# A fused windowed attention and FFN kernel: who sets the ones tile, and the order of loads, units and first FFN chunks in the first half batch

## The chip, the cores and the metric

The kernel runs on one core of a Trainium2 chip. The metric is the device time in microseconds of one execution, as the median of some runs. A profile is one such execution, taken by the hardware profiler; its span reaches from the first instruction to the last and leaves out what lies around it.

Names of the engines in the profile: PE does matmuls and transposes (PEld is its weight load), DVE is VectorE, ACT is ScalarE, POOL is GpSimd, SP only issues DMAs here. ACT and POOL issue some DMAs too.

## The reference

```python
def _attn_ref(q, k, v, n_sink, window):          # q, k, v: (4, 8, 768, 64); n_sink 4, window 128
    scores = 1.0 / np.sqrt(D) * np.matmul(q, k.transpose(0, 1, 3, 2))
    keep = is_sink | in_window                   # key < 4, or 0 <= query - key < 128
    scores = np.where(keep, scores, -1000000000.0)
...
    a = np.exp(scores)
    a = a / (np.sum(a, axis=-1, keepdims=True) + 1e-09)
    return np.matmul(a, v)

def _moe_ref(x, w_in, w_out, beta):              # x: (3072, 512), w_in: (512, 2048), w_out: (2048, 512)
    h = x @ w_in
    g = h * (1.0 / (1.0 + np.exp(-beta * h)))
    return g @ w_out
```

The attention's output, heads side by side, is x. Inputs and the output are float32.

## The kernel before

The work is cut into eight half batches of 384 tokens, and each of these into four units of two heads. A unit passes these steps: its q and k are cast to bfloat16 and transposed on PE (T, line 795, copied out to qkT by ACT or DVE); scores of a burst of tiles (S, line 895) and their exponential on ACT (E, line 913); probabilities times values and the division (A, lines 1000 to 1006); the transpose of the result into xT (R, line 1026). In the first half batch the mask is a bias that PE adds to the scores (line 876); from the second on it is set on E after the exponential, by POOL (line 927) or DVE (lines 921 and 931). From the fourth half batch on the transposes T and R are done by DMA and not by PE. A half batch's x then goes through the FFN: H (line 1053) is four matmuls that make a 128x384 tile of h, followed by tanh on ACT (t, line 1063) and a product on DVE (g, line 1065); O (line 1081) multiplies four g tiles with w_out. Outputs are copied to osb and stored from POOL's queue (line 1099).

In the first half batch values come in another layout, so that they are sorted by nine matmuls with one-hot matrices (V, line 705), of which POOL first casts the values (mix, tile g, line 567). The first four FFN tiles of that half batch (w_in columns 0 to 511) are not made one after the other, but as P0 to P3: P with number c adds the contribution of heads 2c and 2c+1 to all four. They need the weight chunks w0 and w1. B brings the beta of the FFN in.

All PE work stands in one list. For the first half batch this list is written out by hand in `ENTRY` (T0 S0 V0 and so on), for the rest in `ORDER`, one letter each. Where the inputs' loads of the first half batch stand is told by `LOAD0`, the loads that come next (chunks w0 to w7 of w_in, and q, k and three pieces v of the second half batch) by `FIRST`. The loads of q and v of the first half batch are issued by SP, its k by ACT, all else by SP. A planner (`Graph`) then lays out casts, copies and masks on ACT, DVE and POOL by estimated costs (the `ns` of each operation, landings of DMAs from `NQ0`, `NV0` and a list of stalls), and each engine's instructions are written out in the order that the planner gave, with semaphores between them. Which engine does a cast or a copy, and in which order an engine does its work, thus follows from the planner's estimates. No time on the chip does.

Where the planner expects PE to wait in the first half batch, it puts in fillers (line 1301): matmuls of the ones tile with itself, 512 or 256 columns wide, into a bank that nobody reads. The ones tile is written by POOL (line 576), after one of the kS tiles and the bias tiles (lines 588 to 600); identity, one-hot and mask tiles are derived from it. ACT's first activation (line 623) reads it too. Stalls and costs stand in lines 51, 61 and 211, the estimates of the first loads in line 485, the loads themselves in lines 656 and 668. Casts and copies have one helper, so that they stand in lines 565 (ACT), 567 (POOL) and 570 (DVE), told apart by their tiles.

Of the kernel before, what the change touches and what calls it, by code (L numbers as in the profile page):

```python
# [9 lines left out]
B, H, S, D = 4, 8, 768, 64  # L10
# [9 lines left out]
EW = 256 * (NB - 1) + 128  # L20


ENTRY = "T0 S0 V0 T1 S1 V1 T2 S2 A0 A1 V2 V3 A2 R0 T3 S3 R1 P0 A3 B R2 P1 R3 P2 P3"
FIRST = "w0 w1 q k w3 w2 w5 w4 v1 v2 v0 w6 w7"
ORDER = "THHTTTHASHHHSHHSHAHHHAHHOROHOHHRHAHRTROHOAOHSORTOSOOATHOTHHOOHHHOSOHHOHOHRAAARAOHRROSOOHHHAHSOOHHOOHAHHRHHROHRHOROOSRAOOSOOOOHHOHAARHHHHAHOHRHHHHHHOHOOSOOHOHHOOHHSOHOHHHHHHROHHOARSAORHRAORAOOOSOAOROOHHHHHHHHROHOHHHHHHHHRHHHHHHHHOOOOOSOOOOOHHSHHHARHOOHHHHROOHOOOHOOHRRHHHOOHHOHOHOHHOOOOOOOOOOOOOOOOH"
LOG = []
HB0 = "0 1|2 3|4 5|6 7"
LOAD0 = "q0 k0 v0 q1 k1 v1 k3 k2 s q2 v3 v2 q3"
LOOK, AHEAD_W = 4, 8


# [5 lines left out]
class Graph:  # L37
# [10 lines left out]
    WIDE, EARLY = 10, 60000  # L48
    SLACK = 0
    YIELD = 500  # L50
    COLD, WARM = 217, 150

    def __init__(self):
        self.ops = []
        self.writers = {}
        self.readers = {}
        self.last_x = {}
        self.free = {e: 800.0 for e in self.ENGINES}
        self.dma_free = 2500.0
        self.stalls = [(4900.0, 900.0), (14000.0, 700.0), (27000.0, 500.0), (36000.0, 500.0)]  # L60
        self.port = {"gp": 0.0, "dve": 0.0}
        self.taken = {"act": [], "dve": [], "gp": []}
        self.group = 0
        self.filler, self.fill_to = None, 0
# [88 lines left out]
    def place(self, o, at):  # L153
        o.at = at
        if o.eng == "gp" or o.eng == "dve" and o.lock:
            self.port[o.eng] = at + (o.hold if o.dma else o.ns)
        if o.dma:
            self.free[o.eng] = at + o.hold
            self.dma_free = max(self.dma_free, at + 1100) + 1.15 * o.ns
            while self.stalls and self.dma_free > self.stalls[0][0]:  # L160
                self.dma_free += self.stalls.pop(0)[1]
            o.end = self.dma_free + 1000
        else:
            o.end = self.free[o.eng] = at + o.ns

    def at(self, keys):

# [11 lines left out]
    def arrange(self):  # L179
# [28 lines left out]
        todo_pe = list(groups.values())  # L208
        self.free = {e: 800.0 for e in self.ENGINES}
        self.dma_free = 2500.0  # L210
        self.stalls = [(4900.0, 900.0), (14000.0, 700.0), (27000.0, 500.0), (36000.0, 500.0)]
        self.port = {"gp": 0.0, "dve": 0.0}
        new, planned = [], set()

# [17 lines left out]
        while todo_pe or pool:  # L232
            best = None
            wide = self.SKIP if self.free["pe"] > self.EARLY else self.WIDE
            if todo_pe and todo_pe[0][0].group <= self.fill_to:
                wide = self.STRICT
            for i, grp in enumerate(todo_pe[:wide]):
                own = set(map(id, grp))
                if any(id(p) not in planned and id(p) not in own for o in grp for p in o.preds):
                    continue  # L240
                t, off = self.free["pe"], 0.0
                for o in grp:
                    t = max([t] + [p.end + self.HOP - off for p in o.preds if id(p) not in own and p.eng != "pe"])
                    off += o.ns
                if best is None or t < best[0] - self.SLACK:
                    best = (t, "pe", i)
                if t <= self.free["pe"]:
                    break
            by_eng = {}
            for o in pool:  # L250
                opts = []
                for e, (fn, ns) in o.alts.items():
                    t = max(self.free[e], ready(o, e), self.shut(o, e))
                    if o.dma and o.chain != 0:
                        t = max(t, self.dma_free - 3000)
                    opts.append((t + ns, t, e))
                _, t, e = min(opts)
                by_eng.setdefault(e, []).append((t, o))
            first = {}
            for e, c in by_eng.items():  # L260
                t0 = min(c, key=lambda x: x[0])[0]
                first[e] = (t0, max((x for x in c if x[0] <= t0), key=lambda x: x[1].tail)[1])
            if "gp" in first and "dve" in first:
                (tg, og), (td, od) = first["gp"], first["dve"]
                if od.lock and od.tail > og.tail and td < tg + self.YIELD:
                    del first["gp"]
            for e, (t0, o) in first.items():
                if best is None or t0 < best[0]:
                    best = (t0, e, o)
            assert best, "stuck"  # L270
            t, e, what = best
            if e == "pe":
                grp = todo_pe.pop(what)
                late = t + self.PAD if t > self.free["pe"] + 40 else t
                self.fill_by = late
                while self.filler and grp[0].group <= self.fill_to and self.free["pe"] + self.filler[0] <= late:
                    o = self.filler[1]()
                    self.place(o, max([self.free["pe"]] + [p.end + self.HOP for p, _ in o.deps]))
                    new.append(o)
                    if self.free["pe"] > 5000:  # L280
                        self.filler = (self.WARM, self.filler[1])
                if grp[0].group > self.fill_to:
                    self.filler = None
                for o in grp:
                    self.place(o, max([self.free["pe"]] + [p.end + self.HOP for p in o.preds if p.eng != "pe"]))
                    done(o)
            else:
                pool.remove(what)
                what.eng = e
                what.fn, what.ns = what.alts[e]  # L290
                self.place(what, t)
                done(what)
# [142 lines left out]
def _program(nc, G, sb, ps, q, k, v, w_in, w_out, beta, out):  # L435
# [46 lines left out]
    vmix = gt[1][:, :, :].rearrange("p m t -> p (m t)")[:, 0:NK * H * D].rearrange("p (h w) -> p h w", h=H)  # L482
    onehot = [osb[j // 2][:, :].bitcast(BF16)[:, j % 2 * HALF:(j % 2 + 1) * HALF] for j in range(NK)]
    W0, Q2 = [0], 1
    NQ0, NV0, NW2 = (530, 975, 1100)
    WIDE_W, SPL, BQ = 2, ('act','gp'), "sp"
    EARLY, BST, SOON = 4, [1,2,2]+[3]*5, 2200
    LANES, QUADS = [6,7], [5,7]
# [2 lines left out]
    def add(eng, fn, ns, r=(), w=(), x=(), dma=None, after=(), hold=550, chain=None):  # L491
        return G.add(eng, fn, ns, r, w, x, dma, None, after, hold, chain)
# [80 lines left out]


    def consts():
        add("gp", lambda e: e.memset(ones[:, :], 1.0), 150, w=["ones"])  # L576
        add("gp", lambda e: e.affine_select(ident[:, :], ones[:, :], [[1, 128]], ALU.is_equal, 0.0,
                                            base=0, channel_multiplier=-1), 250, r=["ones"], w=["ident"])
        add("gp", lambda e: e.affine_select(ident32[:, :], ones[0:16, 0:16], [[1, 16]], ALU.is_equal, 0.0,
# [206 lines left out]
    def T(u):  # L786

        G.begin()
        hb, hp = u // 4, u % 4
        bs = take(1) + (take(1) if hb < 2 else [])  # L790
        for i, n in enumerate("qk"):
            bk = bs[i % len(bs)]
            mp = P[:, bk, :].bitcast(BF16)[:, i * HALF:(i + 1) * HALF]
# [244 lines left out]
    def HP(c):  # L1038
        G.begin()
        if c == 0:  # L1040
            for m in range(4):
                first_h.extend(take(1))
        for m in range(4):
            HQ(0, m, [first_h[m]], [c])

    def HQ(T_, m, bs=None, cs=range(4)):
# [222 lines left out]
    for x in LOADS[12:N1]:  # L1269
# [10 lines left out]
    ring[0] = None  # L1280
    for x in ENTRY.split():
        i = int(x[1:] or 0)
        if x[0] == "V":
            sort(i)
        elif x == "B":
            beta_in()
        elif x[0] == "P":
            HP(i)
            if i == 3:
                give(first_h)  # L1290
                G.mark_group = G.group
        elif x[0] == "A":
            AV(i)
            done["AV"] += 1
            mark(("onu", i), ("on", i % NON))
        elif x[0] == "R":
            OT(i)
            mark(("xTu", i % 4, i // 4), ("xT", i % 4, i // 4 % NXT))
        else:
            {"T": T, "S": SC}[x[0]](i)  # L1300
    G.fill([lambda e, n=n: e.matmul(P[:, 7, 0:128 * n].rearrange("p (a b) -> p a b", a=n), ones[:, :],  # L1301
                                    ones[:, :].unsqueeze(1).to_broadcast([128, n, 128]), start=True, stop=True)
            for n in (2, 4)], ["ones"])
    give([7])
# [6 lines left out]
    done.update(T=4, SC=len(HB0.split("|")), AV=4, OT=4, H=4, load=N1)  # L1311
# [120 lines left out]
```

## Time and profile before

| | |
|---|---|
| runs | 223.7, 223.72, 222.51 us; median 223.7 |
| the profiled execution | 224.31 us, of which the span is 222.6 us |
| busy share of the span | PE 97%, ACT 67%, DVE 60%, POOL 33% |
| instructions | 4681 |
| DMA | 39.89 MB, 179 GB/s as a mean |
| granted clock of PE | 1.000 |

Busy time of PE counts the fillers. Matmuls are pipelined, so the duration of one is longer than the distance to the next, and costs are better read from differences of starts. A matmul's clock is granted in full all along by the profile's row, but the distance of equal matmuls halves about 7.5 us into the span.

The loads' times from issue to landing, each asked for by itself, give these landings, in us from the span's start. First half batch, on SP: q0 3.9, v0 5.2, q1 6.8, v1 8.1, q2 9.4, v3 9.8, v2 10.3, q3 10.9; on ACT: k0 4.2, k1 5.4, k3 7.9, k2 9.2. Then, on SP: w0 12.4, w1 14.0, q of the second half batch 16.4, its k 19.5, w3 20.8, and w7, the last chunk of w_in, 32.6.

### The profile page before, as it was taken

What the parts mean: (1) busy time and instruction counts of PE and PEld (TensorE: products, weight loads), DVE (VectorE), ACT (ScalarE), POOL (GpSimd) and SP (SyncE); (2) the same over time, 40 slices, a digit from 0 to 9 for tenths busy, and PEclk for the clock granted to TensorE, in tenths of its full rate; (3) what the DMA queues carried; (4) which work ended last, traced back from release to release, by engine and by line L of the source; (5) the groups of instructions that cost most, each with busy time, mean ns of one, the idle gap of its engine ahead of it and who ended that gap; (6) DMA issues with size and microseconds to landing.
All of it is one profiled execution on the core that took longest, in us unless ns stands there. A gap on an engine that the chain in (4) does not pass through costs nothing.

```text
span 222.6 us, 4681 instructions
## 1 busy us (share of the span) xinstructions
PE 215.0 (97%) x1847; PEld 123.7 (56%) x1847; DVE 132.8 (60%) x286; ACT 149.8 (67%) x248; POOL 74.3 (33%) x139
## 2 busy tenths in 40 slices
PE   5999898999999999999999999999999999999995
PEld 2786555455546556545654555646565456455543
DVE  1575989986577535739973647678688007145300
ACT  2587999385985699575776697385886666176421
POOL 7473544000461087256203472083000464000000
PEclk9999999999999999999999999999999999999999
DMA  6999999999989976999958987979769111410112
GB/s 187 332 333 374 215 338 384 348 264 219 199 135 196 219 114 160 176 239 235 186 79 172 230 161 169 181 145 256 108 144 165 47 47 50 94 75 0 47 47 94
DMA packets 92821, 39.89 MB, mean 179 GB/s; under 512 B 79152, under 2 KB 87616, under 8 KB 92800
## 3 DMA queue, kind: packets, MB, share of 16 engines
q1 hardware_dynamic: 90032, 33.31, 69.6%
q0 software_dynamic: 1680, 5.51, 7.7%
q10 hardware_dynamic: 1088, 0.79, 1.1%
q8 instruction: 14, 0.23, 0.5%
q14 instruction: 7, 0.06, 0.1%
HBM read 27.40 MB, written 6.29 MB: 151 GB/s over the span
## 4 chain that ended last, share of the span: by engine, by line
PE 86%; DVE 7%; ACT 4%; POOL 1%; issue 1%; POOLq 0%
PE P L1081 36%; PE P L1053 34%; PE P L1000 4%; PE P L895 4%; PE P L1301 2%; DVE g L1065 2%; ACT E L913 2%; DVE E L931 2%; PE P L876 1%; PE P L795 1%; ACT t L1063 1%; PE P L705 1%; DVE onorm L1006 1%; PE P L1026 1%; DVE w_out L570 1%; ACT qkT L565 1%
## 5 line engine op out<-in xcount | busy, mean ns | idle before, releaser
L1065 DVE SCALAR_TENSOR_TENSOR g<-t,P 128x384 bf16<-128x384 f32 x128 | 68.4, 551 | 53.4 <-ACT t L1063 49.2
L1063 ACT ACTIVATE t<-P,hbeta 128x384 f32<-128x384 f32 x128 | 72.5, 590 | 31.5 <-PE P L1053 25.1
L1053 PE MATMUL P<-xT,w_in 128*128 128x384 bf16 x512 | 91.7, 326 | 1.1 <-DVE w_in L570 0.5
L1081 PE MATMUL P<-w_out,g 128*128 128x512 bf16 (+2 forms) x400 | 91.0, 371 | 0.0
L1053 PEld LDWEIGHTS P<-xT,w_in 128*128 128x128 bf16 x512 | 48.5, 98 | 35.9 <-DVE g L1065 1.2
L1081 PEld LDWEIGHTS P<-w_out,g 128*128 128x128 bf16 x400 | 37.2, 98 | 38.2 <-DVE g L1065 0.8
L927 POOL TENSOR_SCALAR_AFFINE_SELECT E<-E 128x512 bf16<-128x512 bf16 x57 | 38.0, 691 | 31.8 <-ACT E L913 31.3
L913 ACT ACTIVATE E<-P 128x1024 bf16<-128x1024 f32 (+1 forms) x47 | 44.0, 999 | 5.7 <-PE P L895 5.5
L1099 POOL DMA_DIRECT2D out_dram<-osb x21 | 11.8, 562 | 65.1 <-ACT osb L565 61.7
L565 ACT ACTIVATE osb<-P 128x512 f32<-128x512 f32 x20 | 11.9, 597 | 20.7 <-PE P L1081 20.6
L1006 DVE TENSOR_TENSOR onorm<-P,rden 128x384 bf16<-128x384 f32 x32 | 17.5, 553 | 0.7
L1000 PE MATMUL P<-vaug,E 128*128 128x65 bf16 x360 | 15.8, 193 | 0.4 <-DVE E L931 0.4
L1000 PEld LDWEIGHTS P<-vaug,E 128*128 128x128 bf16 x360 | 14.4, 97 | 2.5 <-DVE E L931 0.5
L895 PEld LDWEIGHTS P<-qkT 64*128 64x128 bf16 x296 | 9.6, 94 | 7.1 <-issue 2.4
L895 PE MATMUL P<-qkT 64*128 64x128 bf16 (+1 forms) x296 | 13.5, 229 | 0.0
L570 DVE CAST q<-q_stage 128x512 bf16<-128x512 f32 (+1 forms) x18 | 7.4, 432 | 6.5 <-DMA q_stage<-in_q_dram 6.5
L570 DVE CAST vaug<-v_stage 128x512 bf16<-128x512 f32 x16 | 7.6, 475 | 6.0 <-DMA v_stage<-in_v_dram 6.0
L1301 PE MATMUL P<-ones 128*128 128x512 bf16 (+1 forms) x22 | 7.5, 429 | 2.5 <-POOL ones L576 2.5
L767 POOL TENSOR_TENSOR kS<-qkT,headm 128x8 bf16<-128x8 bf16 (+1 forms) x10 | 2.3, 226 | 21.5 <-ACT qkT L565 19.1
L565 ACT ACTIVATE qkT<-P 128x384 bf16<-128x384 bf16 (+1 forms) x12 | 6.5, 584 | 2.9 <-PE P L795 2.8
L1004 DVE RECIPROCAL rden<-P 128x6 f32<-128x6 f32 x32 | 5.8, 187 | 4.5 <-PE P L1000 4.3
L565 ACT ACTIVATE xT<-P 128x384 bf16<-128x384 bf16 x10 | 5.0, 503 | 4.2 <-PE P L1026 4.2
(70 smaller groups left out, 125.3 us busy)
## 6 DMA issues: line engine op xcount, KB each, us to landing
v_stage<-in_v_dram SPq DMA_DIRECT2D x21, 256.0 KB, 4.6
out_dram<-osb POOLq DMA_DIRECT2D x21, 256.0 KB, 3.0
q_stage<-in_q_dram SPq DMA_DIRECT2D x15, 256.0 KB, 5.1
k_stage<-in_k_dram SPq DMA_DIRECT2D x15, 256.0 KB, 5.1
wst<-in_moe_w_in_dram SPq DMA_DIRECT2D x5, 512.0 KB, 6.6
wst<-in_moe_w_out_dram SPq DMA_DIRECT2D x4, 512.0 KB, 7.4
g<-in_moe_w_out_dram SPq DMA_DIRECT2D x4, 512.0 KB, 8.9
q_stage<-in_q_dram SPq DMA_DIRECT2D x2, 768.0 KB, 8.4
```

The source lines that it names most:

```text
L565: return lambda e: e.activation(dst, src, AF.Copy, bias=0.0, scale=scale)
L570: return lambda e: e.tensor_copy(dst, src)
L895: add("pe", lambda e, dst=dst, kt=kt, kc=kc, rows=rows, q0=q0, nq=nq, u=u: e.matmul(dst, kt[rows, kc:kc + 128], qkT[rows, u % NT, 0, q0:q0 ...
L913: add("act", lambda e, src=src, dst_=dst_: e.activation(dst_, src, AF.Exp, bias=0.0, scale=SCALE), act_ns(256 * ns_), w=[("E", z)] + [("m" ...
L927: alts = {"gp": (lambda e, dd=dd, sg=sg: e.affine_select(dd, dd, [[0, 4], [sg, 128]], ALU.is_ge, 0.0, base=min(sg, 0), channel_multiplier= ...
L1000: e.matmul(A[:, c0:c0 + D + 1], E[t_ % NE][:, i, hh, :], vaug[vz][:, kb % NK, 2 * hp + hh, :], start=a, stop=o, skip_group_check=True), 31,
L1006: add("dve", lambda e: e.tensor_tensor(onorm[on][:, :, :, :].rearrange("p m h d -> p (m h) d"), av[:, :, 0:D], rden[on][:, :].unsqueeze(2) ...
L1053: add("pe", lambda e, c=c: e.matmul(hp, w_in16[:, c, m * 128:(m + 1) * 128], xT[:, c, t0:t0 + HALF], start=(c == 0), stop=(c == 3)), mm_ns ...
L1063: add("act", lambda e: e.activation(tt[ti][:, :], hp, AF.Tanh, bias=0.0, scale=hbeta[:, m:m + 1]), act_ns(HALF) + 93, r=["hbeta"], w=[("t" ...
L1065: add("dve", lambda e: e.scalar_tensor_tensor(gt[T_ % NG][:, m, :], tt[ti][:, :], 1.0, hp, ALU.add, ALU.mult), dve_ns(HALF), r=[("t", ti)] ...
L1081: add("pe", lambda e, m=m: e.matmul(P[:, bk, 0:n], gt[T_ % NG][:, m, t * 128:(t + 1) * 128], w_out16[:, m, cols], start=(m == 0), stop=(m ...
L1301: G.fill([lambda e, n=n: e.matmul(P[:, 7, 0:128 * n].rearrange("p (a b) -> p a b", a=n), ones[:, :], ones[:, :].unsqueeze(1).to_broadcast( ...
```

## The change

The ones tile is set by DVE and not by POOL. `ENTRY`, `FIRST`, `LOAD0` and `ORDER` get other contents of the same kind: all four T, S, V, A, R and P and the B of `ENTRY` are still there, and all loads. Some of the planner's figures are set otherwise (two estimates of load durations, the list of stalls, a doubled duration for PE's groups before 6500 ns, and the time from which fillers are taken as fast). Three names come in, of which `NP` and `TB` have the values that stood there before, and `X` is not used in `ENTRY`; the fillers' call has moved into a function, called at the same place.

```diff
-ENTRY = "T0 S0 V0 T1 S1 V1 T2 S2 A0 A1 V2 V3 A2 R0 T3 S3 R1 P0 A3 B R2 P1 R3 P2 P3"
-FIRST = "w0 w1 q k w3 w2 w5 w4 v1 v2 v0 w6 w7"
+ENTRY = "T0 S0 T1 V0 S1 T2 V1 A0 T3 S2 A1 V2 R0 S3 V3 A2 A3 R1 P0 R3 R2 P1 B P2 P3"
+FIRST = "k w1 w0 q w3 w2 w4 w5 v0 v1 v2 w6 w7"
...
+NP, TB = 4, 2
-LOAD0 = "q0 k0 v0 q1 k1 v1 k3 k2 s q2 v3 v2 q3"
+LOAD0 = "q0 k0 v0 q1 k1 v1 q2 k2 q3 k3 v3 s v2"
...
-    COLD, WARM = 217, 150
+    COLD, WARM, FULL = 217, 150, 6500
...
-        self.stalls = [(4900.0, 900.0), (14000.0, 700.0), (27000.0, 500.0), (36000.0, 500.0)]
+        self.stalls = [(4900.0, 650.0), (17000.0, 600.0), (27500.0, 1100.0), (36000.0, 500.0)]
...
-            o.end = self.free[o.eng] = at + o.ns
+            cold = o.eng == "pe" and at < self.FULL and getattr(o, "group", None) is not None
+            o.end = self.free[o.eng] = at + o.ns * (1 + cold)
...
-                    if self.free["pe"] > 5000:
+                    if self.free["pe"] > self.FULL:
...
-    NQ0, NV0, NW2 = (530, 975, 1100)
+    NQ0, NV0, NW2 = (500, 920, 1100)
...
-        add("gp", lambda e: e.memset(ones[:, :], 1.0), 150, w=["ones"])
+        add("dve", lambda e: e.memset(ones[:, :], 1.0), 150, w=["ones"])
...
-        bs = take(1) + (take(1) if hb < 2 else [])
+        bs = take(1) + (take(1) if hb < (2 if u > 3 or TB == 2 else 0) else [])
```

`ORDER` is a string of some 300 letters, nearly all of whose places differ. What the planner makes of all this: 17 fillers and not 22 (nine of 512 and one of 256 columns ahead of T0, four of 512 and three of 256 later); k2, k3 and their load issues behind ACT's first activation, together with k1; q2 cast by ACT, k3 by POOL; of the eight casts of w_out two on ACT, six on DVE and none on POOL (before: one, five and two); of the last six casts of w_in three on DVE and three on POOL (before: two and four); of the masks of the second half batch eight on DVE and four on POOL (before: nine and three).

More of the change, by code (lines that the diff above doesn't have):

```diff
@@ L20 @@
 EW = 256 * (NB - 1) + 128
-ENTRY = "T0 S0 V0 T1 S1 V1 T2 S2 A0 A1 V2 V3 A2 R0 T3 S3 R1 P0 A3 B R2 P1 R3 P2 P3"
-FIRST = "w0 w1 q k w3 w2 w5 w4 v1 v2 v0 w6 w7"
-ORDER = "THHTTTHASHHHSHHSHAHHHAHHOROHOHHRHAHRTROHOAOHSORTOSOOATHOTHHOOHHHOSOHHOHOHRAAARAOHRROSOOHHHAHSOOHHOOHAHHRHHROHRHOROOSRAOOSOOOOHHOHAARHHHHAHOHRHHHHHHOHOOSOOHOHHOOHHSOHOHHHHHHROHHOARSAORHRAORAOOOSOAOROOHHHHHHHHROHOHHHHHHHHRHHHHHHHHOOOOOSOOOOOHHSHHHARHOOHHHHROOHOOOHOOHRRHHHOOHHOHOHOHHOOOOOOOOOOOOOOOOH"
+ENTRY = "T0 S0 T1 V0 S1 T2 V1 A0 T3 S2 A1 V2 R0 S3 V3 A2 A3 R1 P0 R3 R2 P1 B P2 P3"
+FIRST = "k w1 w0 q w3 w2 w4 w5 v0 v1 v2 w6 w7"
+ORDER = "TTTHAHTSHHHSHHAHHSRHHHOOAOHAHARRHHHTRRHHAOOOHOHOTTOSOOSHTOHHOHHOSHOAOOHAHAOHHHRRRAOROSOAHSHOOOHHAHHHHRHRORHRHHOHSROOOOSOOORHOOOAHAHHHHHHRHAAHHHHOHHOOSOHHHHOOOHHOOOHOHHHSOHHHOHHRHSAOAOOORSOORAOOORHRHHHARHHHRHHHHHHHHHOHAHHHHHOOHHORHOOOOSOOOHHOHHHHHHSOHAHHOHHOOHHROOOROOHROOOOHOOOOOROHOHOHHHOOOOOOOOHO"
 LOG = []
+NP, TB = 4, 2
 HB0 = "0 1|2 3|4 5|6 7"
-LOAD0 = "q0 k0 v0 q1 k1 v1 k3 k2 s q2 v3 v2 q3"
+LOAD0 = "q0 k0 v0 q1 k1 v1 q2 k2 q3 k3 v3 s v2"
 LOOK, AHEAD_W = 4, 8
@@ L210, in arrange @@
         self.dma_free = 2500.0
-        self.stalls = [(4900.0, 900.0), (14000.0, 700.0), (27000.0, 500.0), (36000.0, 500.0)]
+        self.stalls = [(4900.0, 650.0), (17000.0, 600.0), (27500.0, 1100.0), (36000.0, 500.0)]
         self.port = {"gp": 0.0, "dve": 0.0}
@@ L1040, in HP @@
         if c == 0:
-            for m in range(4):
+            for m in range(NP):
                 first_h.extend(take(1))
-        for m in range(4):
+        for m in range(NP):
             HQ(0, m, [first_h[m]], [c])
@@ L1280, in _program, with stop_fill @@
     ring[0] = None
+    def stop_fill():
+        G.fill([lambda e, n=n: e.matmul(P[:, 7, 0:128 * n].rearrange("p (a b) -> p a b", a=n), ones[:, :],
+                                        ones[:, :].unsqueeze(1).to_broadcast([128, n, 128]), start=True, stop=True)
+                for n in (2, 4)], ["ones"])
+        give([7])
     for x in ENTRY.split():
@@ L1286, in _program @@
             beta_in()
+        elif x == "X":
+            stop_fill()
         elif x[0] == "P":
@@ L1300, in _program @@
             {"T": T, "S": SC}[x[0]](i)
[L1301 to L1304, printed above, removed]
+    if 7 in held:
+        stop_fill()
     for x in LOADS[12:N1]:
@@ L1310, in _program @@
     ring[0] = None
-    done.update(T=4, SC=len(HB0.split("|")), AV=4, OT=4, H=4, load=N1)
+    done.update(T=4, SC=len(HB0.split("|")), AV=4, OT=4, H=NP, load=N1)
     n_cast[0], n_w[0] = 20, sum(isinstance(x, int) for x in LOADS[:N1])
```

## The prediction, made before the changed kernel ran

> **What bounds it now.** I read the busy time by stages first. Columns: stretch, its length, then busy time (instructions) of PE, PEld, DVE, ACT, POOL, granted clock, DMA share, GB/s.
>
> ```profile
> core 0: us, PE busy (x) PEld busy (x) DVE busy (x) ACT busy (x) POOL busy (x), PEclk, DMA share, GB/s
> 0.00:2.46 2.46, 0.00 (x0) 0.00 (x1) 0.00 (x0) 0.60 (x1) 1.51 (x9) 1.00 0.17 38
> 2.46:22.20 19.74, 19.74 (x223) 13.43 (x224) 11.00 (x28) 12.61 (x23) 11.57 (x33) 1.00 1.07 340
> 22.20:27.00 4.80, 3.95 (x40) 2.43 (x39) 4.41 (x9) 4.73 (x11) 2.81 (x3) 1.00 1.06 237
> 27.00:45.00 18.00, 16.53 (x177) 9.84 (x177) 17.21 (x36) 13.61 (x23) 5.14 (x7) 1.00 1.01 344
> ...
> 51.00:222.60 171.60, 168.76 (x1379) 94.62 (x1377) 95.07 (x203) 113.06 (x184) 53.26 (x88) 1.00 0.72 141
> ```
>
> From 51 us on PE works for 168.8 of 171.6 us, and 2.5 of the rest is the tail behind its last matmul. So the time is PE's work plus what PE loses before 51. In 22-27 ACT is full (4.73 of 4.80), in 27-45 DVE (17.21 of 18), and the DMA engines are full up to 51. PE's loss at the start shows in its timeline (start, length, instructions; in brackets the idle time before and who ended it):
>
> ```profile
> 2.46 3.38 PE L1301 MATMUL P<-ones 128*128 128x512 bf16 x8 [2.46 <-POOL ones L576]
> 5.64 0.53 PE L795 MATMUL P<-ident,q 128*128 128x128 bf16 x3
> ...
> 8.70 0.59 PE L1301 MATMUL P<-ones 128*128 128x512 bf16 x2
> 9.13 0.33 PE L795 MATMUL P<-ident,q 128*128 128x128 bf16 x3
> ...
> 24.09 0.34 PE L795 MATMUL P<-ident,k 128*128 128x128 bf16 x3 [0.59 <-DVE g L1065]
> ...
> 31.52 1.47 PE L1053 MATMUL P<-xT,w_in 128*128 128x384 bf16 x8 [0.17 <-DVE g L1065]
> ...
> 34.06 0.82 PE L1053 MATMUL P<-xT,w_in 128*128 128x384 bf16 x4 [0.52 <-DVE w_in L570]
> ...
> 38.37 0.26 PE L1000 MATMUL P<-vaug,E 128*128 128x65 bf16 x3 [0.40 <-DVE E L931]
> ...
> 42.12 0.34 PE L1026 MATMUL P<-ident,onorm 128*128 128x128 bf16 x3 [0.19 <-DVE onorm L1006]
> ```
>
> PE stands until POOL has set the ones tile, and up to 22 us the L1301 fillers stand where it would wait. By differences of starts a 512-column filler costs 0.43 while the clock is low (the eight: 3.18) and 0.22 later (8.70 to 9.13: 0.43 for two). Some were not needed: the second unit's casts end at 7.74, its transposes start at 9.13. Why DVE is late in 27-45 shows on DVE and POOL:
>
> ```profile
> 32.54 0.42 DVE L931 TENSOR_TENSOR E<-E,osb 128x512 bf16<-128x512 bf16 x1
> 37.05 1.26 DVE L931 TENSOR_TENSOR E<-E,osb 128x512 bf16<-128x512 bf16 x1
> 38.92 0.74 DVE L931 TENSOR_TENSOR E<-E,osb 128x512 bf16<-128x512 bf16 x1
> ```
>
> ```profile
> 36.99 1.05 POOL L567 TENSOR_SCALAR_AFFINE_SELECT w_out<-g 128x1024 bf16<-128x1024 f32 x1 [0.40 <-DMA g<-in_moe_w_out_dram]
> 38.34 1.05 POOL L567 TENSOR_SCALAR_AFFINE_SELECT w_out<-g 128x1024 bf16<-128x1024 f32 x1 [0.30 <-DMA g<-in_moe_w_out_dram]
> ```
>
> The same mask takes 0.42 alone, and 1.26 and 0.74 beside POOL's two w_out casts: it ends 0.27 after the cast does, both times.
>
> **The change, part by part.** I laid the changed order of each engine end to end with these durations: each instruction at the later of its engine's last end and its producers' ends, each load at the landing of the same place in the line.
>
> *Ones on DVE.* POOL's took 0.20, behind kS and two bias tiles. DVE shows nothing before 3.88, but SP, ACT and POOL start at 0.80. For 128 columns its nearest rows are 0.16 (hbeta, 16 columns) and 0.36 (xT, 384). Ones stands at about 1.0, PE starts at 1.05 instead of 2.46: -1.4 (-1.2 to -1.45). ACT's warm-up, which waits for ones, releases the issues behind it earlier: k2's goes at 1.9 (2.87 before), k3's at 2.4 (2.44).
>
> *Fillers.* Before: 3.18 ahead of the first unit, one of 0.21, later 2.06 by differences of starts, 5.45 in all. In the changed order nine of 512 and one of 256 stand ahead of the first unit (9 x 0.43 + 0.21 = 4.06), then four of 512 and three of 256 (4 x 0.22 + 3 x 0.11 = 1.19): 5.25, so -0.2. The head ends at 5.1; the casts that T0 needs end at 4.83.
>
> The matmul spacing halves at 7.5, 5.0 after PE's first matmul; by that row it would now halve at 6.1, with T0 and half of S0 slow as T0 and most of S0 were: -0.1, inside the range. The Trainium skill (TensorE: Matmul & The Clock Gate, What's actually happening) has the gate watch a free-running window of 3.4 us, so the turn could come anywhere from 4.5 to 7.9 (an estimate from that page); by that the entry would differ by at most some 0.3, most of it taken up by the wait for q2 that follows.
>
> *Loads and units to 22 us.* All instructions of the entry stay: four each of T, S, V, A, R, P. Loads share one full line, so places land where they did (3.9, 5.2, 6.8, 8.1, 9.4, 9.8, 10.3, 10.9 on SP). q2 keeps 9.4, but ACT now casts it, behind two exponentials: to 9.8. PE, at S1's end near 9.4, waits 0.5 (0 to 1.0). Short waits for ACT and DVE copies, some 0.1 each, stand in both orders alike. k of the second half batch (768 KB, 2.4) goes ahead of w1 and w0, which land at 14.9 and 16.4 instead of 14.0 and 12.4. POOL's casts (1.06 and 0.62) end near 17.1, when PE, by its own sum, reaches P0 at 17.3 (18.1 - 1.2, and 0.4 for A3, which now stands ahead): cover of 0.2, taken as nothing, up to +0.7 if a landing slips as k's did (3.1 instead of 2.4). q lands last, at k's 19.5, cast before PE is through P3. Entry: -1.4 - 0.2 - 0.1 + 0.5 = **-1.2** (-1.7 to -0.2). SP waits for nothing before its issue at 25.04, so no queue is moved.
>
> *22 to 27.* The next weights land as before (20.8 on), and ACT is full. Laid out, PE waits for bank releases and g 0.5, 0.6 and 0.9 in place of 0.85 (1.3 with restarts): **+0.9**, most of the entry's gain (0 to +1.2).
>
> *27 to 45.* POOL's two w_out casts go to ACT and DVE (ACT 2 of 8, was 1; DVE 6, was 5), and DVE gets one w_in cast more, in its free time before 27. So the 0.84 and 0.32 that the masks lost go, a cast of 0.69 comes, and a mask goes to POOL (-0.42): DVE -0.9. PE's waits at 31.52, 38.37 and 42.12 hang on that queue; PE loses 2.3 here: idle 1.47 in six waits, and some 0.07 to 0.17 for each restart. Laid out, of them stays the one for the w_in chunk that lands at 32.6, 0.75 to 0.9; the others go, as FFN groups stand ready where PE stood: **-1.5** (0 to -2.0).
>
> *After 45.* One wait at 62.29 (0.32, with its restart 0.48) for a DVE g: it goes with DVE's earlier end: **-0.4** (0 to -0.5). The tail stays. NP, TB and X keep the old values or are unused; the planner's figures act only through the order.
>
> Sum: -1.2 + 0.9 - 1.5 - 0.4 = **-2.2**. This is against the profiled execution, 224.3 (span 222.6 and 1.7 around it), 0.6 above the median of 223.7: 222.1 for it, **221.5** for the median.
>
> **Rivals.** *Given back.* ACT, DVE and DMA are full from 22 to 45; if the landings of w_in and w_out set the pace there, an earlier PE only waits longer, and only the masks' loss (-0.4 at 38.37) stays: 223.3 (222.8 to 223.9). For: DMA share 1.0 to 51. Against: PE's waits there are put down to DVE, once alone to a cast whose weights had just landed. A DVE that starts late, so that ones is no earlier, ends here too.
>
> *Slower: DVE and POOL collide more.* Before, POOL's stage 27-45 holds 5.1 us, and cost DVE some 2.1 (the two masks, and casts of 1.12 and 1.15 instead of 0.68 beside POOL's masks). After it, POOL has four masks and a w_in cast, 3.6 us; each can hold a DVE cast or mask for its whole length. If all do, DVE loses 3.6, 1.5 more than before, on the queue that sets the pace, and the two casts bring nothing: -1.2 + 0.9 + 1.5 = +1.2, **224.9**. It decides against the change from about 2.4 us of such losses. The Trainium skill (SBUF — State Buffer, Who interferes with whom) calls the port pair that DVE and GpSimd share an exclusive lock; the trace agrees, with 1.26 for 0.42. Against: before, only two fifths of POOL's time struck.
>
> **Numbers.** Forecast 0.72, given back 0.18, slower 0.10. The forecast's own range is 220.1 to 222.8; the whole, 220.1 to 223.9, leaves out most of the slower case and the ends. A measurement of this kernel tells about 1% (2.2 us) from no change: somewhat over half of the forecast's case (0.40) lies beyond it, as what I took for 22-27 is nearer to its upper end; the rest of it (0.32), the second case and a part of the third make 0.53 within; 0.07 slower.
>
> **What would show it.** PE's first L1301 at 1.0 to 1.2; T0 at 5.1 to 5.3; a PE wait of about 0.5 ahead of the third unit; P3's end near 21.0; idle PE of 1.5 to 2 in 21-27; under 1.0 of idle in 27-45, with one wait for DVE w_in near 33; no mask above 1.0. Wrong if P0 waits for w_in past 18, if POOL's L927 stretches DVE's casts, or if idle time after 45 grows.

## The result, and the profile after

| | median, us | runs | span of the profiled execution, us | its time, us |
|---|---|---|---|---|
| before | 223.65 | 20 (222.28 to 224.41) | 222.6 | 224.31 |
| changed | 221.89 | 20 (221.31 to 224.27) | 219.8 | 221.49 |

The medians differ by 1.8 us. The ratio is 0.9941 (95% interval 0.992 to 0.9961): by it the change takes away 0.6%, 1.3 us (0.9 to 1.8). The forecast was 2.2. The two profiled executions differ by 2.8. They overstate it: that of before lies 0.66 above its median, that of after 0.4 below.

The busy time by stages, with the columns of the forecast's view (stretch, length, busy time and instructions of PE, PEld, DVE, ACT, POOL, granted clock, DMA share, GB/s):

```profile
core 0: us, PE busy (x) PEld busy (x) DVE busy (x) ACT busy (x) POOL busy (x), PEclk, DMA share, GB/s
1.10:21.00 19.90, 19.05 (x217) 12.21 (x217) 10.41 (x26) 13.35 (x23) 12.03 (x37) 1.00 1.03 320
21.00:27.00 6.00, 4.90 (x55) 2.97 (x54) 5.35 (x11) 5.96 (x14) 2.65 (x3) 1.00 1.00 257
27.00:45.00 18.00, 17.65 (x175) 10.97 (x174) 15.98 (x37) 14.51 (x24) 3.85 (x6) 1.00 1.04 351
45.00:51.00 6.00, 6.00 (x40) 3.50 (x39) 5.86 (x14) 5.37 (x11) 0.66 (x1) 1.00 1.06 238
```

From 27 to 45 us PE is idle for 0.35 us where it was idle for 1.47. ACT is as full from 21 to 27 as it was, DVE has more slack from 27 to 45 (15.98 for 17.21), the DMA share there is much the same (1.04 for 1.01). PE's own timeline (start, length, instructions; in brackets the idle time before and who ended it):

```profile
1.12 4.23 PE L1284 MATMUL P<-ones 128*128 128x512 bf16 x10 [1.12 <-DVE ones L578]
5.15 0.53 PE L797 MATMUL P<-ident,q 128*128 128x128 bf16 x3
...
18.02 0.81 PE L1055 MATMUL P<-xT,w_in 128*128 128x384 bf16 x4 [0.71 <-POOL w_in L569]
...
21.32 0.33 PE L797 MATMUL P<-ident,q 128*128 128x128 bf16 x3
...
22.52 0.34 PE L797 MATMUL P<-ident,q 128*128 128x128 bf16 x3 [0.37 <-ACT qkT L567]
...
26.79 1.47 PE L1055 MATMUL P<-xT,w_in 128*128 128x384 bf16 x8 [0.47 <-DVE g L1067]
...
33.48 0.82 PE L1055 MATMUL P<-xT,w_in 128*128 128x384 bf16 x4 [0.35 <-DVE w_in L572]
```

(Lines of the changed kernel are higher by two: T is L797, the FFN's H L1055, the casts L567, L569 and L572. The fillers, whose call has moved, are L1284.) After the wait at 33.48 PE has no wait of 0.15 us or more up to 66 us. Before, it had waits at 34.06, 38.37, 42.12 and 62.29. The gain along the program, as PE's time less the work it has done (distances of starts beyond the usual distance of the same pair, so that restarts count), stands at -0.9 when the second half batch begins (21.32 for 22.22), falls to -0.35 at 27 us, and is -2.4 at 45 and -2.9 after 62 us.

### The profile page after: what moved, and what is told of

It is laid out like the page before. It is cut to its first block, busy times and chain, and to the rows that moved or that the text cites. A ratio compares the mean times of both kernels' runs of the same rounds, so it can differ in the third digit from the quotient of the medians.

```text
span 219.8 us, 4670 instructions
## 1 busy us (share of the span) xinstructions
PE 213.9 (97%) x1842; PEld 122.9 (56%) x1842; DVE 134.4 (61%) x293; ACT 148.6 (68%) x246; POOL 70.2 (32%) x135
## 4 chain that ended last, share of the span: by engine, by line
PE 84%; SPq 11%; DMA 3%; issue 1%; DVE 0%; ACT 0%
PE P L1083 38%; PE P L1055 35%; SPq L658 6%; SPq L670 4%; PE P L1002 4%; PE P L897 4%; DMA wst<-in_moe_w_in_dram 3%; PE P L990 1%; PE P L797 1%; PE P L1028 1%; PE P L945 1%; SPq L1273 0%; DVE w_in L572 0%; SPq L748 0%; PE P L974 0%
## 5 line engine op out<-in xcount | busy, mean ns | idle before, releaser
L1055 PE MATMUL P<-xT,w_in 128*128 128x384 bf16 x512 | 90.6, 326 | 1.7 <-POOL w_in L569 0.7
L1055 PEld LDWEIGHTS P<-xT,w_in 128*128 128x128 bf16 x512 | 48.7, 98 | 36.5 <-POOL w_in L569 1.0
L929 POOL TENSOR_SCALAR_AFFINE_SELECT E<-E 128x512 bf16<-128x512 bf16 x58 | 38.8, 692 | 51.6 <-ACT E L915 51.1
L567 ACT ACTIVATE osb<-P 128x512 f32<-128x512 f32 x15 | 9.0, 600 | 20.7 <-PE P L1083 20.4
L573 DVE TENSOR_SCALAR osb<-P 128x512 f32<-128x512 f32 x8 | 5.5, 688 | 9.4 <-PE P L1083 9.4
L923 DVE TENSOR_TENSOR E<-E,maskS 128x512 bf16<-128x512 bf16 x12 | 6.2, 529 | 5.5 <-ACT E L915 5.5
L569 POOL TENSOR_SCALAR_AFFINE_SELECT vaug<-v_stage 128x512 bf16<-128x512 f32 x3 | 2.0, 661 | 23.5 <-DMA v_stage<-in_v_dram 23.5
L567 ACT ACTIVATE qkT<-P 128x384 bf16<-128x384 bf16 (+1 forms) x12 | 6.5, 579 | 4.0 <-PE P L797 4.0
L572 DVE CAST vaug<-v_stage 128x512 bf16<-128x512 f32 x16 | 7.8, 498 | 1.0 <-DMA v_stage<-in_v_dram 1.0
L572 DVE CAST q<-q_stage 128x512 bf16<-128x512 f32 (+1 forms) x13 | 5.5, 437 | 4.5 <-DMA q_stage<-in_q_dram 4.4
```

Of the source, the lines that this page charges most:

```text
L567: return lambda e: e.activation(dst, src, AF.Copy, bias=0.0, scale=scale)
L572: return lambda e: e.tensor_copy(dst, src)
L929: alts = {"gp": (lambda e, dd=dd, sg=sg: e.affine_select(dd, dd, [[0, 4], [sg, 128]], ALU.is_ge, 0.0, base=min(sg, 0), channel_multiplier= ...
L1055: add("pe", lambda e, c=c: e.matmul(hp, w_in16[:, c, m * 128:(m + 1) * 128], xT[:, c, t0:t0 + HALF], start=(c == 0), stop=(c == 3)), mm_ns ...
```

## The experiments

Twelve kernels were run. The time before, measured with them, was 223.45, 223.52 and 223.73 in the three groups, so the ratios are what can be compared between them.

| kernel | what differs | median, us | ratio to before (95%) |
|---|---|---|---|
| changed, again | nothing | 222.19 | 0.9929 (0.9908 to 0.9951) |
| ones_back | changed, ones on POOL | 222.05 | 0.9943 (0.9919 to 0.9968) |
| ones_only | before, ones on DVE | 223.23 | 0.9987 (0.9966 to 1.0008) |
| act_casts | before, POOL's two w_out casts on ACT | 223.26 | 0.9996 (0.9971 to 1.002) |
| pool_casts | changed, two w_out casts on POOL | 222.23 | 0.9951 (0.9927 to 0.9975) |
| old_order | changed, `ORDER` of before | 222.57 | 0.9962 (0.9937 to 0.9988) |
| old_loads | changed, `LOAD0` of before | 223.28 | 0.9978 (0.9961 to 0.9995) |
| old_units | changed, `ENTRY` of before | 224.42 | 1.0037 (1.002 to 1.0054) |
| old_firsts | changed, `FIRST` of before | 225.56 | 1.0087 (1.0062 to 1.0111) |
| old_entry | changed, all three of before | 224.45 | 1.0053 (1.0032 to 1.0074) |
| w_first | changed, w1 and w0 ahead of k | 222.62 | 0.9967 (0.9942 to 0.9992) |
| late4 | changed, last four w_out casts on POOL | 222.13 | 0.9924 (0.9903 to 0.9945) |

**The ones tile.** ones_back takes the new ones tile out of the changed kernel, as below; ones_only puts it alone into the kernel before, the other way round.

```diff
-        add("dve", lambda e: e.memset(ones[:, :], 1.0), 150, w=["ones"])
+        add("gp", lambda e: e.memset(ones[:, :], 1.0), 150, w=["ones"])
```

> The changed kernel with the ones tile set by POOL again, nothing else undone; the planner then puts 14 fillers and not 17. Theory of the prediction (the earlier start is a gain of its own, -1.4): PE starts at 2.4, P3 and all that follows stand later, the entry loses 1.0 to 1.4 and, with most of that given back at 22 to 27, the time is 0.3 to 1.0 us above the changed kernel. Rival (the first unit is tied to its casts, which end near 4.8, and fillers only fill the time up to there): the first unit's transposes start at 5.1 to 5.5 as before, only the clock turns later (first unit and its scores slow, some 0.5 us), and the time is within 0.3 us of the changed kernel.

> The kernel before with the ones tile set by DVE, nothing else changed; the planner puts 24 fillers and not 22. Theory of the prediction: PE starts at 1.1, the second half batch is reached up to 1 us earlier, half or more of it is given back at 22 to 27, and the time falls by 0.3 to 0.7 us against the kernel before. Rival (first unit tied to its casts): first unit at 5.1 to 5.6, time the same within 0.3 us.

PE's timeline of ones_back begins:

```profile
2.46 3.17 PE L1284 MATMUL P<-ones 128*128 128x512 bf16 x7 [2.46 <-POOL ones L578]
5.42 0.51 PE L797 MATMUL P<-ident,q 128*128 128x128 bf16 x3
```

PE starts 1.34 later than in the changed kernel and its first transposes come only 0.27 later, because the planner puts seven fillers of 512 columns ahead of them and not nine and one of 256. The casts that these transposes need end at 5.00 in the changed kernel and at 5.26 here, 0.15 ahead of the transposes in both, so an earlier PE could not have begun them much earlier. Most of an early start is filled up with fillers, and the time is the same (222.05, beside 221.89 and 222.19 for the changed kernel). Alone, the new ones tile gives 0.3 us, give or take 0.5, which does not part the two expectations of ones_only.

**POOL's casts.** The forecast put the gain from 27 to 45 us down to them. act_casts edits the kernel before as below; pool_casts edits the same line of the changed kernel, with `if j < 4 or j in (10, 11)` for POOL.

```diff
-        any_of(copies(dst, src_, {"act": 947} if j in W0 else {"gp": 1060} if j < 4 else {"act": 947, "dve": 602, "gp": 1060}), r=[("wst", j % NWS)], w=[("w16", m, h)], lock=True)
+        any_of(copies(dst, src_, {"act": 947} if j in W0 or j in (10, 11) else {"gp": 1060} if j < 4 else {"act": 947, "dve": 602, "gp": 1060}), r=[("wst", j % NWS)], w=[("w16", m, h)], lock=True)
```

> The other direction: the kernel before, with its two POOL casts of w_out (chunks 10 and 11) put on ACT. By the prediction's step TensorE's loss between 27 and 45 us falls by 1.0 to 1.5 and the time is 222.0 to 222.6. Rival: the masks return to 0.42, but ACT, which is over 80% busy there, gets 1.9 us more to do and hands its exponentials and t over later; the waits change their releaser from DVE or POOL to ACT, and the time is 223.3 to 223.8, as before.

> The changed kernel with two casts of w_out (chunks 10 and 11, which it has on ACT and DVE) put on POOL, where the kernel before had two. By the prediction's step for 27 to 45 us (POOL's casts stretch DVE's masks from 0.42 to 0.74 and 1.26, and TensorE then waits for R and the units behind), TensorE's loss between 27 and 45 us grows by 1 to 1.5 us and the time to 223.0 to 223.4. Rival: the stretched masks are real and cost DVE about 1.2 us, but DVE has 2 us of slack there, so that TensorE gives up 0.3 to 0.4 and the time is 222.0 to 222.3. A third: the gain from 27 to 45 us is of the order of the units alone, and the time stays within 0.2 of the changed kernel's.

DVE's and PE's timelines of act_casts:

```profile
36.17 0.85 DVE L931 TENSOR_TENSOR E<-E,osb 128x512 bf16<-128x512 bf16 x1
37.63 0.41 DVE L931 TENSOR_TENSOR E<-E,osb 128x512 bf16<-128x512 bf16 x1
```

```profile
33.64 0.82 PE L1053 MATMUL P<-xT,w_in 128*128 128x384 bf16 x4 [0.51 <-DVE w_in L570]
42.22 0.34 PE L1026 MATMUL P<-ident,onorm 128*128 128x128 bf16 x3 [0.25 <-DVE onorm L1006]
61.10 0.82 PE L1053 MATMUL P<-xT,w_in 128*128 128x384 bf16 x4 [0.32 <-DVE g L1065]
```

The mask at 37.63 takes 0.41; one beside POOL's own mask (35.54 to 36.74) still takes 0.85. PE's wait for the mask at 38.37 is gone, that ahead of R at 42 has grown by 0.06, those for w_in and near 61 stay. By distances of starts PE loses 1.2 less up to 45 us than in the profile of before, 0.4 of it by an earlier turn of the clock (6.7 for 7.5); but the medians differ by 0.3, and the ratio's interval reaches 0.65 us below the time before and 0.45 above it. In the other direction POOL cast w_out at 36.64 and 38.66 and hardly a mask was held, as the planner had put them elsewhere:

```profile
35.93 0.38 DVE L933 TENSOR_TENSOR E<-E,osb 128x512 bf16<-128x512 bf16 x1
38.09 0.46 DVE L933 TENSOR_TENSOR E<-E,osb 128x512 bf16<-128x512 bf16 x1
```

Its time is that of the changed kernel (222.23 beside 222.19 in the same group). So POOL's casts are worth some tenths by the medians, 0.65 at the end of act_casts' interval, and not most of the 1.5 of the forecast. What a held mask costs by itself was not isolated: pool_casts did not bring one back.

**The orders.** All five kernels are the changed one with lists of before put back: `ORDER` in old_order, and of the three lists below `ENTRY` in old_units, `FIRST` in old_firsts, `LOAD0` in old_loads and all three in old_entry.

```diff
-ENTRY = "T0 S0 T1 V0 S1 T2 V1 A0 T3 S2 A1 V2 R0 S3 V3 A2 A3 R1 P0 R3 R2 P1 B P2 P3"
+ENTRY = "T0 S0 V0 T1 S1 V1 T2 S2 A0 A1 V2 V3 A2 R0 T3 S3 R1 P0 A3 B R2 P1 R3 P2 P3"
-FIRST = "k w1 w0 q w3 w2 w4 w5 v0 v1 v2 w6 w7"
+FIRST = "w0 w1 q k w3 w2 w5 w4 v1 v2 v0 w6 w7"
-LOAD0 = "q0 k0 v0 q1 k1 v1 q2 k2 q3 k3 v3 s v2"
+LOAD0 = "q0 k0 v0 q1 k1 v1 k3 k2 s q2 v3 v2 q3"
```

> The changed kernel with the ORDER of before (the entry, the loads and the ones tile stay changed). Theory of the prediction (what is won lasts in 27 to 45 us, and hangs on which engine casts w_out and in which order FFN groups stand): PE's waits of 27 to 45 come back, 1.0 to 2.0 us above the changed kernel, near the kernel before. Rival (the earlier entry itself makes DVE and ACT earlier, the order matters little): within 0.5 us of the changed kernel.

> The changed kernel with ENTRY, FIRST and LOAD0 of before (ORDER, the planner's figures and the ones tile stay changed). Theory of the prediction (the entry's gain is mostly given back at 22 to 27): 0.3 to 0.8 us above the changed kernel. Rival (ORDER was laid out for this entry, and with another the casts and groups fall in other places): PE waits again in 27 to 63 us, 2 to 3.5 us above the changed kernel, and so above the kernel before.

> The changed kernel with only the order of the half batch's first loads (q, k, v by group) put back to that of before; the order of the units, of the first list and of the rest stay. It parts the entry's gain, which is 2.5 us against the kernel with all three orders put back (224.45). If the loads carry it (T1 and T2 wait for k1 or q2 when their transfers come in the old order, and the waits last), the time is 223.5 to 224.5, most of it as new waits at 23 to 36 us. If the order of the units carries it, the time is 222.0 to 222.7.

> The changed kernel with only the order of the first half batch's units put back to that of before; the loads and the rest stay. If the units' order carries the gain, the time is 223.7 to 224.7: units stand ahead of others whose operands land earlier, and a wait of 1 us or more comes back at 23 to 28 us. If the loads carry it, 222.0 to 222.7. If neither does so by itself, and each is right only with the other laid out to it, both this kernel and the one with the old loads lose 1.5 us or more, and the two losses together are more than the 2.5 that putting back all of it cost.

> The changed kernel with only the order of the next loads (the list that begins with w_in's chunks and the second half batch's q and k) put back to that of before. P0 then has its chunk of w_in 2 us or more ahead and does not wait (0.7 in the changed kernel), but q and k of the second half batch land about 2 us later, and T4 and T5 behind them. By the prediction's term for k ahead of w (T4 at 21.3 for 22.2) the loss shows at 22 to 24 us and lasts: 222.6 to 223.4. Rival: it is made up by P0's 0.7, and the time is 221.8 to 222.3. Against both: with q and k later, casts pile up behind them, and waits of 0.5 to 1 us come at 28 and at 58 to 62 us; 224 or more.

Against the changed kernel (0.9935 as the mean of its two ratios), old_order costs 0.6 us, which is not clear of the noise (some 0.7), old_loads 1.0, old_units 2.3, old_firsts 3.4, and all three of the entry together 2.6. So old_order lies between its two expectations, old_entry is where its rival had it, old_units lies in the range for a units' order that carries the gain, and old_loads falls just short of the same range for the loads. No run puts the planner's other figures (the stalls and the estimates of loads) back, so their share is not known. The parts do not add up: 1.0, 2.3 and 3.4 make 6.7 where all three together cost 2.6, and two of the lists make the kernel slower than the one before when they alone are put back. The expectation for old_firsts that went farthest, waits at 28 and at 58 to 62 us, is the one that held:

```profile
29.29 1.48 PE L1055 MATMUL P<-xT,w_in 128*128 128x384 bf16 x8 [0.74 <-DVE g L1067]
...
59.84 0.82 PE L1055 MATMUL P<-xT,w_in 128*128 128x384 bf16 x4 [0.88 <-ACT E L915]
62.05 0.39 PE L897 MATMUL P<-qkT 64*128 64x256 bf16 x6 [0.71 <-ACT qkT L567]
```

What such a misfit can look like is plainest in old_loads. It begins the second half batch 0.14 us later than the changed kernel (21.46 for 21.32), so its loads hold up hardly any unit ahead of that. Its longest wait comes at 26.62:

```profile
24.12 0.55 DVE L1067 SCALAR_TENSOR_TENSOR g<-t,P 128x384 bf16<-128x384 f32 x1
25.41 0.69 DVE L572 CAST w_in<-g 128x1024 bf16<-128x1024 f32 x1 [0.74 <-DMA g<-in_moe_w_in_dram]
26.02 1.01 DVE L1067 SCALAR_TENSOR_TENSOR g<-t,P 128x384 bf16<-128x384 f32 x2
```

```profile
26.62 0.34 PE L797 MATMUL P<-ident,k 128*128 128x128 bf16 x3 [1.49 <-DVE g L1067]
```

DVE stands for 0.74 until a chunk of w_in lands, casts it, and only then makes the g that releases the bank which PE's next transposes need. PE's wait is put down to g. It begins at 25.13 and takes in the last 0.28 of DVE's wait, the cast and the g. In the changed kernel the same stretch of DVE reads:

```profile
24.45 0.68 DVE L572 CAST w_in<-g 128x1024 bf16<-128x1024 f32 x1
25.05 0.54 DVE L1067 SCALAR_TENSOR_TENSOR g<-t,P 128x384 bf16<-128x384 f32 x1
25.57 0.69 DVE L572 CAST w_in<-g 128x1024 bf16<-128x1024 f32 x1
26.18 1.01 DVE L1067 SCALAR_TENSOR_TENSOR g<-t,P 128x384 bf16<-128x384 f32 x2
```

The g at 25.05 goes ahead of the cast of the chunk that lands last (25.55), and DVE does not stand in this stretch. old_order shows it a second time:

```profile
40.73 0.69 DVE L572 CAST w_out<-wst 128x1024 bf16<-128x1024 f32 x1 [1.41 <-DMA wst<-in_moe_w_out_dram]
41.34 0.19 DVE L1006 RECIPROCAL rden<-P 128x6 f32<-128x6 f32 x1
41.56 0.56 DVE L1008 TENSOR_TENSOR onorm<-P,rden 128x384 bf16<-128x384 f32 x1
```

```profile
42.18 0.34 PE L1028 MATMUL P<-ident,onorm 128*128 128x128 bf16 x3 [1.04 <-DVE onorm L1008]
```

DVE waits 1.41 for a chunk of w_out, the product onorm stands behind the cast until 41.56, and PE waits 1.04 for it. (This profiled execution also lost 0.88 ahead of the second unit's q, which landed at 7.5 and not at 6.4.) old_units has the same pattern: DVE waits 0.44 for w_in up to 25.58, two g stand behind the cast, and PE waits 1.89 for them at 27.25. It does not account for old_firsts: no cast of DVE waits for a landing ahead of the g of 29.29, and the two other waits shown are for ACT.

**The changed kernel once more.** No edit.

> The changed kernel itself, once more. It sets the bar for the other three of this batch, and it tests two readings of its first profile. If the 0.71 us that P0's matmuls waited at 18.02 for w_in's first chunk was a slip of that chunk's transfer in one execution, this profile shows P0 without it, or with another length, while the waits that belong to the order (0.37 at 22.5 for ACT's qkT, 0.47 at 26.8 for DVE's g, 0.35 at 33.5 for DVE's cast of w_in) stay. If it belongs to the order, it is there again at 0.6 to 0.8. The turn of the granted clock, 5.6 us in the first profile against 7.5 in the kernel before, should move between executions by up to a microsecond if it is not set by the program. Time 221.5 to 222.2.

P0's wait is there again:

```profile
17.98 0.81 PE L1055 MATMUL P<-xT,w_in 128*128 128x384 bf16 x4 [0.67 <-POOL w_in L569]
```

The chunk landed at 17.2 both times. But the order alone does not set this: in ones_back and pool_casts, with the same three lists, it landed at 16.3 and 16.4, and P0 did not wait. The turn of the clock came at 5.6 again, while in pool_casts, whose first fillers are the same, it came at 6.5. On PE the two profiled executions of the changed kernel agree to 0.1 us up to 46 us. Then the second loses 0.8:

```profile
43.22 0.69 DVE L572 CAST w_out<-wst 128x1024 bf16<-128x1024 f32 x1 [0.73 <-DMA wst<-in_moe_w_out_dram]
44.82 0.69 DVE L572 CAST w_out<-g 128x1024 bf16<-128x1024 f32 x1 [0.91 <-DMA g<-in_moe_w_out_dram]
45.43 0.69 DVE L754 TENSOR_TENSOR vS<-vS,own 128x512 bf16<-128x512 f32 x1
46.03 1.47 DVE L1067 SCALAR_TENSOR_TENSOR g<-t,P 128x384 bf16<-128x384 f32 x3
```

```profile
46.64 1.47 PE L1055 MATMUL P<-xT,w_in 128*128 128x384 bf16 x8 [0.20 <-DVE g L1067]
```

A chunk of w_out landed at 39.09 where it had landed at 38.43, all behind it came later, and the g behind the last cast began at 46.03 for 45.22 in the first profile. That is the same queue again, and the rows put it down to one transfer that slipped.

**The last casts on POOL.** This is the version that should beat the changed kernel if such slips matter.

```diff
+LATE = (12, 13, 14, 15)
...
-        any_of(copies(dst, src_, {"act": 947} if j in W0 else {"gp": 1060} if j < 4 else {"act": 947, "dve": 602, "gp": 1060}), r=[("wst", j % NWS)], w=[("w16", m, h)], lock=True)
+        any_of(copies(dst, src_, {"act": 947} if j in W0 else {"gp": 1060} if j < 4 or j in LATE else {"act": 947, "dve": 602, "gp": 1060}), r=[("wst", j % NWS)], w=[("w16", m, h)], lock=True)
```

> The changed kernel with its last four casts of w_out (chunks 12 to 15) put on POOL; DVE has them in the changed kernel, in order with its work on g. Two profiled executions of the changed kernel agree to 0.02 us up to 46 us and then differ by 0.8: in the second, one transfer of w_out slipped by 0.66 us (39.09 for 38.43), the four casts behind it each came 0.5 to 0.8 later, g stood behind them on DVE (46.03 for 45.22) and TensorE waited 0.36 at 46.64 and 0.27 at 50.55. If slips of this kind, held by DVE's order, are a good part of the changed kernel's spread and of its median, the four casts on POOL, which has nothing else between 36 and 44 us, free g from the landings: the wait at 46.6 is gone whether or not a transfer slips, and the time is 221.2 to 221.8. Rival: POOL's casts of 1.05 us hold the last chunk later than DVE's of 0.69 did, POOL's work on the sinks comes later behind them, or the slip reaches TensorE by another way; the time is 221.9 to 222.5.

It is not told apart from the changed kernel (0.9924 beside 0.9929 and 0.9941). POOL's rows, and DVE's:

```profile
44.53 1.05 POOL L570 TENSOR_SCALAR_AFFINE_SELECT w_out<-g 128x1024 bf16<-128x1024 f32 x1 [0.43 <-DMA g<-in_moe_w_out_dram]
```

```profile
44.77 1.35 DVE L755 TENSOR_TENSOR vS<-vS,own 128x512 bf16<-128x512 f32 x1 [0.31 <-DMA vS<-in_v_dram]
46.05 2.40 DVE L1068 SCALAR_TENSOR_TENSOR g<-t,P 128x384 bf16<-128x384 f32 x5
```

(The lines are higher by one more.) DVE no longer waits for w_out. But its product with two inputs, vS, which takes 0.69 in the changed kernel, takes 1.35 beside POOL's cast, and the g behind it starts at 46.05, as late as with the slip. w_out's landing is out of DVE's queue, and POOL has taken its place there. PE's wait at 46.6 is gone all the same, as the expectation had it, and the time did not fall with it. This profiled execution had begun its second half batch 0.45 later than the changed kernel's (21.77 for 21.32), after a wait of 0.81 ahead of the third unit.

**P0's chunk ahead of k.**

```diff
-FIRST = "k w1 w0 q w3 w2 w4 w5 v0 v1 v2 w6 w7"
+FIRST = "w1 w0 k q w3 w2 w4 w5 v0 v1 v2 w6 w7"
```

> The changed kernel with w_in's first two chunks asked for ahead of the first k unit's data in the list of first loads, so that P0's cover does not depend on when they land. If the wait at 18.02 (0.71) is a loss that lasts, TensorE is 0.7 earlier from P0 on and the time is 221.0 to 221.3. Rival: what the entry gains is given back at the next wait for ACT or DVE (22.5 and 26.8), as with half of what it gained already, and the time is 221.7 to 222.2. Against both: k lands later and T1 or S0 waits for it, 0.3 to 0.6, and the time is 222.0 to 222.5.

P0 does not wait, and the time is no better: 222.62 beside 222.19 in its group, above all three expectations. The profiled execution can't show what became of P0's 0.7, since it lost 1.36 ahead of the third unit's q (10.74), behind a load of k that landed at 8.3 and not at 6.7. late4, with the loads of the changed kernel, had the same slip and waited 0.81 there. ones_back shows more: P0 did not wait there, the second half batch began at 20.72 and not at 21.32, and its span is 219.5 for 219.8, so about half of these 0.6 us was given back.

## Why the forecast held, and which of its steps did not

The time, its range and the forecast's side were right (221.5 forecast, 221.9 measured). The steps under it were right less often, and that the number came so near is partly luck: the terms as measured in the profile add up to -2.9 and not to -2.2, and the changed kernel's profile lies 0.4 below its median, for which the forecast had no term.

- **Ones, -1.4.** The size of the row was right (1.12 for 2.46), its worth was not. Undone in the changed kernel it costs nothing that can be measured. The forecast had the reason in its hand, "the casts that T0 needs end at 4.83": the start of PE's work is tied to its data, and what the early ones tile bought, beside the 0.27 above, was three more fillers (two of 512 columns and one of 256, 1.07).
- **Fillers, -0.2, and the clock's turn at 6.1, -0.1.** T0 came at 5.15, as summed. The clock turned at 5.6, 4.5 after PE's first matmul; in the kernels that start PE at 1.12 it turned between 5.1 and 6.5, so that a turn carried over from one execution was a guess within a range. By the free-running window of the Trainium skill (TensorE: Matmul & The Clock Gate, What's actually happening) it could, as an estimate, have been 4.5 to 7.9, which these agree with.
- **Wait of 0.5 for q2's cast.** It did not come (T2 at 9.41 without a wait): q2 landed at 8.5, not 9.4. In two other executions with the same `LOAD0` (late4, w_first) it did, at 0.81 and 1.36, behind a slip of k2. Over the kernels with this `LOAD0` q2 landed between 8.4 and 10.1, so the size of this term was open to chance.
- **P0's cover of 0.2, up to +0.7 without it.** The cover was gone in both executions of the changed kernel: w0 landed at 17.2 and PE waited 0.71 and 0.67. Where it landed at 16.3 and 16.4 (ones_back, pool_casts) there was no wait. With P0 at 18.02 one of the forecast's own signs of being wrong came; it stood for the +0.7 that the range held. Entry: -0.9 and not -1.2.
- **22 to 27, +0.9 given back.** +0.55. The part given back was there, with ACT full and waits for ACT's qkT and DVE's g, as laid out, but smaller: PE was idle for 1.10 from 21 to 27 and not for 1.5 to 2.
- **27 to 45, -1.5.** The place was right and PE gained 2.06 there; one wait for DVE's w_in near 33 stayed, as said, and the rest was under 1.0. **The step's cause failed**: the two POOL casts, taken out of the kernel before, brought no measurable gain, and put back they cost none. What the runs show in its place is that no single list carries the gain: each of the three of the entry, put back alone, costs 1.0 to 3.4. In three of the misfits a cast that waits for a landing stands in DVE's queue ahead of a g or an onorm for which PE waits (DVE's waits of 0.74, 1.41 and 0.44 stand behind PE's of 1.49, 1.04 and 1.89). The waits of the kernel before are of another kind. Its DVE waits for no landing from 27 to 45 us and is simply full, as the forecast read it; ahead of 42.12 its rows follow one another without a gap:

```profile
39.59 1.47 DVE L1065 SCALAR_TENSOR_TENSOR g<-t,P 128x384 bf16<-128x384 f32 x3
40.98 0.18 DVE L1004 RECIPROCAL rden<-P 128x6 f32<-128x6 f32 x1
41.09 0.50 DVE L1065 SCALAR_TENSOR_TENSOR g<-t,P 128x384 bf16<-128x384 f32 x1
41.52 0.54 DVE L1006 TENSOR_TENSOR onorm<-P,rden 128x384 bf16<-128x384 f32 x1
```

The casts were a part of that queue, but without them (act_casts: DVE 16.54 of 18) only the wait at 38.37 went. Which part of the new order makes up the rest of the 2.06 stays open.
- **After 45, -0.4.** -0.5; the wait at 62.29 is gone. In the second execution of the changed kernel a slipped transfer took 0.8 back there.
- **From the execution to the median, 0.6.** The forecast took this off, and rightly. The other half of it, that the changed kernel's executions spread as well, was missing: of the 2.8 between the two profiles, the second profile of the changed kernel (span 220.5 for 219.8) gives 0.7 back.

Of the rivals, "given back" was nearest to what happened to the ones tile and to the entry: ACT, DVE and the landings set the pace from 22 us on, and there an earlier PE is worth only a part of its lead (0.9 became 0.35; ones_back's 0.6 became 0.3). It fell as a forecast because PE gained more from 27 to 45 us than it allowed. "Slower, by collisions of DVE and POOL" did not come to pass: POOL worked 3.85 us from 27 to 45 us, no mask on DVE took more than 0.42 there, and its cast of w_in beside POOL's masks took 0.78 for 0.69. The price that it named is real: late4 paid 0.66 for a single one (1.35 for 0.69).

## What to carry to other kernels

A wait that the profile puts down to an engine's product may belong to a DMA: go back along that engine's queue to the next cast that waits for a landing, and see whether the product can go ahead of it. Moving the casts to another engine is no sure way: late4 did that and gained nothing that can be measured. An engine's early start is worth only what the data behind it allow; before counting it, look up when the first real operands are ready. Lists that were laid out together have to be tested together, since one of them put back alone was worse than all.

## What the hardware showed that was not expected

**The clock fell in mid-kernel.** In the profiled execution of old_units the granted clock was halved from 28.99 to 32.41. The two stretches before and the one of the fall:

```profile
22.17:25.58 3.41, 1.82 (x15) 1.04 (x14) 2.49 (x7) 3.18 (x8) 2.10 (x2) 1.00 1.05 241
25.58:28.99 3.41, 1.74 (x25) 1.08 (x26) 2.48 (x5) 2.39 (x5) 0.00 (x0) 1.00 0.85 179
28.99:32.41 3.42, 3.42 (x21) 1.62 (x20) 2.36 (x6) 3.02 (x6) 0.00 (x0) 0.50 1.03 363
```

PE had been idle for 1.89 ahead of 27.25, inside a stretch of 3.41 in which it was busy for 1.74, 51%. The clock had turned up at 5.10, and 28.99 is seven such stretches later. In old_loads a stretch on its own grid (23.10 to 26.51, from its turn at 6.03) had PE busy for 1.81, 53%, and kept the clock. The Trainium skill (TensorE: Matmul & The Clock Gate, HAM oscillation — how this bites in real kernels) puts the rule as "no PE-idle gaps >~3.4µs". This trace differs: no wait of PE ahead of the fall was longer than 1.89 us. Both executions would fit a gate that looks at the busy share of each stretch, with a line between 51% and 53%. They would as well fit one that falls after two weak stretches in a row, since the stretch before in old_units was at 53% too and old_loads had a single one. No run tells these apart. A run of the changed kernel itself, the slowest of its 20 (224.27), shows a mean clock of 0.992, the same as that execution; the others show 0.999 or 1.0.

**Landings slip.** The same loads in the same order landed up to 1.6 us apart between executions (k2 at 6.7, 6.9 and 8.3). A slip can move what stands behind it: in the second profile of the changed kernel the rest of w_out came 0.66 to 0.82 later. It need not: a chunk of w_in slipped there too (31.20 for 30.59), and the next one landed on time (32.56 for 32.61). The spread of the changed kernel's runs, 221.3 to 223.1 without that slowest run, is of the size that two such slips of 0.8 would cost; that they make it was not shown.
